# Attention and a two-layer product on one Trainium2 core: loads of five head pairs and weight pieces moved, and one unit's attention outputs and output product rearranged

## The chip, the cores and the metric

The kernel runs on one core of one Trainium2 chip. A core has five engines, each with its own instruction stream: TensorE (PE: matmuls; its weight loads are shown as PEld), VectorE (DVE), ScalarE (ACT), GpSimd (POOL) and SyncE (SP, which here only issues DMA). DMA is issued from SP's and from POOL's streams. An engine takes its instructions in order and waits on semaphores for what other engines and DMAs produce. Matmuls write into PSUM, which has eight banks of 2 KB per partition; DVE, ACT and POOL move data on from there or from SBUF.

The metric is the device time of one execution in microseconds (us), as the median of several runs. A profiled execution gives the trace of every instruction; its span reaches from the first to the last instruction, and its own time is a little longer.

## The reference

Attention over 8 batches, 12 heads, 448 tokens and 64 columns per head, and then a product with an elementwise function and a second product over all 3584 tokens:

```python
# q, k, v: (8, 12, 448, 64)
scale = 1.0 / np.sqrt(q.shape[-1])
scores = scale * np.matmul(q, k.transpose(0, 1, 3, 2))
m = np.max(scores, axis=-1, keepdims=True)
e = np.exp(scores - m)
attn = e / (np.sum(e, axis=-1, keepdims=True) + np.exp(-m) + 1e-09)
attn_out = np.matmul(attn, v)

x = attn_out.transpose(0, 2, 1, 3).reshape(8 * 448, 768)
h = x @ w_in                                  # (768, 2048)
sp = np.where(h > 20.0, h, np.log1p(np.exp(np.minimum(h, 20.0))))
g = h * np.tanh(sp)                           # mish
return g @ w_out                              # (2048, 768)
```

Inputs and output are float32; the kernel computes its matmuls in bf16.

## The kernel before

**Pairs, units, steps.** Two heads form a pair: 48 pairs, six per batch. Three pairs form a unit (`UNIT_PAIRS`), two units a batch (`UNITS_PER_B`). Pairs 0 to 5 are done in a head loop of their own. The main loop runs over u = 2, 3, ... (so u=4 is the fifth unit of pairs and u=5 the sixth). Each u has an attention block of 12 steps (n = 0 to 11: three pairs with four steps each, `STEPS`) and then an MLP block of eight tiles (f = 0 to 7). The attention block of u handles pairs 3u to 3u + 2; the MLP block of u handles batch (u − 2) // 2, whose attention has been done by then.

**A step.** `scores` multiplies q and k for two row tiles into one of three score tiles of PSUM (two banks each: sc0, sc1, sc2) and DVE takes the negative row maximum (L293). `exps` lets ACT take the exponentials (L306) into the bf16 buffer en and sum them. `scores_ahead` keeps up to three score tiles in use ahead of the exps. The remaining two PSUM banks (mo0, mo1) are handed out by `mo_take`, first free first, to everything else.

**Normalise and turn.** `denominators` forms the reciprocal of the sum. `normalise` scales en's seven tiles: by DVE (L341), by POOL (L339, `on_pool`, for the third pair of a unit), or shared in the head (tiles 0 to 3 by POOL, 4 to 6 by DVE). POOL reads its own copy of the reciprocals, rden2, which DVE makes (L331). en is then turned into eT, for most pairs by a DMA transpose on SP's queue (L345), for pairs 2, 4, 5, 6 and 7 by TensorE (`turn_on_pe`, L356, `BY_PE`). The three pairs of a unit are normalised in its MLP block, at f = 0, 3 and 4.

**Attention outputs.** `av_pair` multiplies eT and v in eight matmuls (L382), into a mo bank or into a bank it is given, and appends the copy to xT (L391) to a list, `late`, that `flush_late` empties at the next step. From u=4 on `av_with` is set: the output of the pair three back is put in at the last step of the current pair (`s == STEPS - 1`), in `scores`, into the second bank of the score tile, which that step does not use. That tile is free once the exps three steps earlier have read it. In u=2 and u=3 the table `AV_AT` puts the outputs at the ends of given steps, into mo banks. At u=4 the three outputs are those of pairs 9, 10 and 11.

**First product.** `mm1_mish`: six matmuls of xT with a tile of w_in (L406), then mish on ACT (L412). The bank is a mo bank, or for f = 1 the first score tile's. `transpose_pair` (L193) and `evac_qk` (L214, L227) prepare the next unit's q and k in the MLP block at f = 1, 3 and 5.

**Second product.** `mm2_part(g, i, q0, nq)`: row tile i (128 rows) of the two batches 2g and 2g + 1, and nq quarters of 192 columns from q0: 16 matmuls (L472) in eight chunks, a mo bank, and a copy by DVE (L459). `plan` lists which parts run in which u, from `first_mm2` = 4 on, as filler in the attention block: after the exps of step n the chunks due by `weight` (5.2 at n = 0, 1.0 for n = 1 to 8, 0.4 for the last three) are issued. Row tile 3 takes its rows from two batches; `gather_mid` (L422, DVE) copies 64 rows of each into one tile, mid, at the end of the unit with the batch's last first-product tiles.

**Queues.** SP's queue takes, in program order: `load_pair` (q, k and v of a pair, 224 KB each, L132), the DMA transposes, and the stores. Loads of pair p0 + 4, p0 + 5 and p0 + 6 (p0 = 3u) are issued at n = 0, 3 and 6 (`LOAD_AT`); there are four buffers for each of q, k and v. POOL's queue takes the casts to bf16 (`cast_pair` at n = 0, 3, 6, of the pair loaded before: L175, L176, L162), its share of the normalising, small copies, and the DMA issues of the weight pieces (`load_w`, L158): 12 pieces of w_in (256 KB), then 8 of w_out (384 KB; 12 to 15 are the first half of its columns, 16 to 19 the second). `W_AT` gives the steps of u = 2, 3 and 4 at which a piece is issued; in u=2 one more is issued at f = 2 and at f = 6.

Of the kernel before, what the change touches and what calls it, by code (L numbers as in the profile page):

```python
# [19 lines left out]
def kernel(  # L20
# [9 lines left out]
    nc = tc.nc  # L30
# [10 lines left out]
    NTILE = 2 * S // 128  # L41
    UNITS_PER_B = HP // UNIT_PAIRS
# [69 lines left out]
    def flush_late():  # L112
        while late:
            late.popleft()()
# [8 lines left out]
    def load_pair(p, which="qkv"):  # L123
        if p >= N_PAIRS:
            return
        b, h0 = p // HP, (p % HP) * 2
        tiles = loaded.setdefault(p, [])
        for nm, src in (("q", q), ("k", k), ("v", v)):
            if nm not in which:
                continue  # L130
            t = ld_pool.tile([SP_, 2, NT * D], FP32, tag=f"{nm}_f", name=f"{nm}_f")
            nc.sync.dma_start(  # L132
                out=t, in_=src[b, h0 : h0 + 2].rearrange("h (p t) d -> p h (t d)", t=NT)
            )
            tiles.append(t)
# [19 lines left out]
    def load_w(n):  # L155
        for _ in range(min(n, len(pieces))):
            dst, src = pieces.popleft()
            nc.gpsimd.dma_start(out=dst, in_=src.rearrange("(a p) c -> p a c", p=128))  # L158
# [80 lines left out]
    def scores_ahead(limit):  # L239

        while rg["next"] < limit and rg["used"] < len(sc_tiles):
            rg["used"] += 1
            scores(rg["next"])
            rg["next"] += 1
# [73 lines left out]
    def denominators(st):  # L318
        nc.vector.scalar_tensor_tensor(
            out=st["den"], in0=st["sums"], scalar=1e-9, in1=st["expm"],  # L320
            op0=ALU.add, op1=ALU.add,
        )
        nc.vector.reciprocal(out=st["rden"], in_=st["den"])

    def normalise(p, dma=True, on_pool=False, shared=0):
        st = att[p]
        en = st["en"]
        if on_pool or shared:

            st["rden2"] = st_pool.tile([128, NTILE], FP32, tag="rden2", name="rden2")  # L330
            nc.vector.tensor_copy(out=st["rden2"], in_=st["rden"])  # L331
        for i in range(NTILE):
            pool_does = on_pool or i < shared
            args = dict(
                out=en[:, :, i, 0:SP_], in0=en[:, :, i, 0:SP_],
                scalar1=st["rden2" if pool_does else "rden"][:, i : i + 1],
            )
            if pool_does:
                nc.gpsimd.tensor_scalar(scalar2=1.0, op0=ALU.mult, op1=ALU.mult, **args)  # L339
            else:  # L340
                nc.vector.tensor_scalar(scalar2=None, op0=ALU.mult, **args)  # L341
        eT = eT_pool.tile([128, NT, 2 * S], BF16, tag="eT", name="eT")
        st["eT"] = eT
        if dma:
            nc.sync.dma_start_transpose(  # L345
                out=eT.rearrange("c j (i q) -> c (j i) q", q=128),
                in_=en.rearrange("q j i c -> q (j i c)"),
            )
# [64 lines left out]
        if not spare:  # L413
            mo_free.append(h_ps)

    def gather_mid(b):

        g, half = divmod(b, 2)
        if half == 0:
            mids[g] = mid_pool.tile([128, FF_T, 128], BF16, tag="mid", name="mid")  # L420
        at = S - 64 if half == 0 else 0
        nc.vector.tensor_copy(  # L422
            out=mids[g][:, :, 64 * half : 64 * half + 64], in_=gT[b][:, :, at : at + 64]
        )

# [59 lines left out]
    first_mm2 = 2 * UNITS_PER_B  # L485

    def whole(g, i):
        return [(g, i, 0, 2), (g, i, 2, 2)]
# [3 lines left out]
    plan = {}  # L492
    for g in range(B // 2):
        u0 = first_mm2 + 4 * g
        rest = plan.pop(u0, [])
        if g == 0:
            plan[u0] = [(0, i, 0, 2) for i in range(2)] + [(0, 2, 0, 1)]
            plan[u0 + 1] = [(0, 2, 1, 1)] + [(0, i, 2, 2) for i in range(3)]
        else:
            plan[u0] = rest + whole(g, 0) + [(g, 1, 0, 1)]  # L500
            plan[u0 + 1] = [(g, 1, 1, 1), (g, 1, 2, 2)] + whole(g, 2)
        plan[u0 + 2] = [(g, 4, 0, 2), (g, 4, 2, 1)] + whole(g, 3)
        plan[u0 + 3] = [(g, 4, 3, 1)] + whole(g, 5) + [(g, 6, 0, 2)]
        if g < B // 2 - 1:
            plan[u0 + 4] = [(g, 6, 2, 2)]
        else:
            plan[u0 + 3] += [(g, 6, 2, 1), (g, 6, 3, 1)]
# [4 lines left out]
    BY_POOL = 4  # L512
    LEAD = UNIT_PAIRS + 1
    LOAD_AT = (0, 3, 6)
    LAST_AV_AT = (0, 6, 9)
    HEAD = HP

# [9 lines left out]
    }  # L527
    AV_HEAD = {(3, 3): 0, (4, 2): 2, (4, 3): 1}
    W_HEAD = {0: 3, 1: 1, 3: 1, 4: 1}
    AV_AT = ({3: 4, 7: 3, 9: 5}, {5: 6, 8: 7, 10: 8})  # L530

    W_AT = ({5: 1, 9: 1}, {1: 1, 4: 1, 5: 1, 7: 1, 9: 1, 11: 1}, {3: 1, 5: 1, 7: 1, 9: 1})
    for which in ("qk", "v"):
        for p in range(UNIT_PAIRS):
            load_pair(p, which)
# [12 lines left out]
    for p in range(HEAD):  # L548
        for s in range(STEPS):
# [20 lines left out]
            if (p, s) in AV_HEAD:  # L570
                av_pair(AV_HEAD[p, s], act=True)
    denominators(att[HEAD - 1])
    normalise(HEAD - 1, dma=HEAD - 1 not in BY_PE, shared=BY_POOL)

    for u in range(UNITS_PER_B, N_UNITS + 2 * UNITS_PER_B):
        attn = u < N_UNITS
        filler = deque()
        for part in plan.get(u, []):
            filler.extend(mm2_part(*part))
        total, done, acc = sum(w for _, w in filler), 0, 0.0  # L580
        p0 = u * UNIT_PAIRS
        if attn and u >= first_mm2:
            av_with.update({p0 + i: p0 + i - UNIT_PAIRS for i in range(UNIT_PAIRS)})
        end = min((u + 1) * UNIT_PAIRS, N_PAIRS) * STEPS

        for n in range(steps):
            pi, s = divmod(n, STEPS)
            p, idx = p0 + pi, p0 * STEPS + n
            late_tp = u == UNITS_PER_B and n == STEPS
            if late_tp:  # L590
                transpose_pair(p0 + 2)
            exps(idx)
            if late_tp:
                evac_qk(p0 + 2)
            if u == UNITS_PER_B + 1:
                for part in TURN_AT[1].get(n, []):
                    turn_on_pe(*part)
            flush_late()
            acc += weight[n]
            want = int(total * acc / sum(weight) + 1e-6)  # L600
            while done < want:
                fn, w = filler.popleft()
                fn()
                done += w
            scores_ahead(end)
            if n in LOAD_AT:
                load_pair(p0 + LOAD_AT.index(n) + LEAD)
                cast_pair(p0 + LOAD_AT.index(n) + LEAD - 1)
            if u - UNITS_PER_B < len(AV_AT):
                early = AV_AT[u - UNITS_PER_B]  # L610
                if n in early:
                    av_pair(early[n])
                if u == UNITS_PER_B:
                    for part in TURN_AT[0].get(n, []):
                        turn_on_pe(*part)
            elif u == N_UNITS and n in LAST_AV_AT:
                av_pair(p0 - UNIT_PAIRS + LAST_AV_AT.index(n))
            if u - UNITS_PER_B < len(W_AT):
                load_w(W_AT[u - UNITS_PER_B].get(n, 0))
        assert done == total  # L620

        moe = u < N_UNITS + UNITS_PER_B
        b, w = (u - UNITS_PER_B) // UNITS_PER_B, u % UNITS_PER_B
        nxt = p0 + UNIT_PAIRS
        todo = sorted(range(p0, nxt), key=lambda p: p in BY_PE)
        for f in range(FF_U):
            if moe:
                mm1_mish(b, w * FF_U + f)
            if u == UNITS_PER_B and f in (2, 6):
                load_w(1)  # L630
            if not attn:
                continue
            if f == 0:
                denominators(att[p0]["whole"])
                normalise(todo[0], dma=todo[0] not in BY_PE)
            if f in (1, 3, 5):
                transpose_pair(nxt + f // 2, bank=f // 2 % 2)
                evac_qk(nxt + f // 2)
            if nxt < DIAG_FROM and f in (4, 6):
                scores_ahead(nxt * STEPS + f // 2 - 1)  # L640
            if f == FF_U - 1:
                scores_ahead(min(nxt * STEPS + 3, N_PAIRS * STEPS))
            if f == 3:
                normalise(todo[1], dma=todo[1] not in BY_PE)
            if f == 4:
                normalise(todo[2], dma=todo[2] not in BY_PE, on_pool=True)
        if attn and u + 1 < N_UNITS:

            nc.scalar.activation(out=one, in_=zero, func=AF.Exp)
        if moe and w == UNITS_PER_B - 1:  # L650
            gather_mid(b)
    flush_late()
    assert not pieces and all(have == 4 for _, have in o_sbs.values())
# [30 lines left out]
```

## Time and profile before

| | |
|---|---|
| Median of three runs | 480.3 us (480.15 to 481.88) |
| The profiled execution's own time | 479.95 us |
| Its span, first to last instruction | 478.0 us |
| Instructions in the span | 8924 |
| Mean granted TensorE clock | 0.982 |
| PE busy (3064 matmuls) | 443.1 us |
| ACT busy | 350.0 us |
| DVE busy | 339.1 us |
| POOL busy | 181.1 us |

A page of the profile gives first the busy time of each engine, then 40 equal slices of the span in which a digit is the busy share in tenths, the granted TensorE clock (PEclk, also in tenths of full speed) and the DMA engines' share. Then comes the chain of work that ended last, followed back from the last instruction. An answer of the trace for windows gives, for stretches of the span, each engine's busy time with its number of instructions in brackets, the granted clock, the DMA share and the rate. A timeline row gives start, duration, engine, source line, operation, output and inputs, shape, the number of instructions put together, and in square brackets the engine's idle time in front and what ended it. Line numbers are those of the kernel before; in the changed kernel the lines behind `normalise` are six or more higher.

### The profile page before, as it was taken

The page shows a single profiled execution, that of the slowest core. Times are in us where ns is not written, and L with a number is a line of the kernel's source. Part 1 is how long each engine was busy: PE and PEld are TensorE (multiplying, and loading weights), DVE is VectorE, ACT ScalarE, POOL GpSimd, SP SyncE. Part 2 cuts the span into 40 slices and gives each one's busy share as a digit, 9 for nine tenths or more (in the row PEclk, how much of TensorE's full clock was granted, in tenths as well). Part 3 has the DMA queues.
Part 4 walks back from the last instruction along what each step waited for, and adds up shares of the span by engine and source line. Part 5 has one row for each costly group of instructions (what it writes and reads, how often), then busy time and mean ns, then how long its engine had stood idle before and what let it go on. Part 6 is the DMA issues. An engine that isn't in the chain of part 4 may idle for free.

```text
span 478.0 us, 8924 instructions
## 1 busy us (share of the span) xinstructions
PE 443.1 (93%) x3064; PEld 248.6 (52%) x3064; DVE 339.1 (71%) x680; ACT 350.0 (73%) x919; POOL 181.1 (38%) x315
## 2 busy tenths in 40 slices
PE   4565888898999999999999999999999999999997
PEld 2233544454655555555555555556555555556565
DVE  4888987968787886878687878788787869420021
ACT  5979678878787888979787878888897978412300
POOL 4877809255514334353535242433535340300000
PEclk9998798899999999999999999999999999999999
DMA  8999969999999989899999999899989595870113
GB/s 228 220 233 220 235 100 234 162 187 238 207 217 276 206 212 219 213 203 246 193 250 182 225 167 228 211 207 234 201 233 212 156 178 127 135 164 24 43 28 105
DMA packets 202381, 90.37 MB, mean 189 GB/s; under 512 B 159072, under 2 KB 198880, under 8 KB 202336
## 3 DMA queue, kind: packets, MB, share of 16 engines
q1 hardware_dynamic: 194848, 83.51, 81.3%
q0 software_dynamic: 7488, 6.29, 8.6%
q8 instruction: 24, 0.39, 0.3%
q14 instruction: 21, 0.17, 0.1%
HBM read 45.61 MB, written 11.01 MB: 118 GB/s over the span
## 4 chain that ended last, share of the span: by engine, by line
PE 76%; ACT 10%; DVE 9%; issue 2%; DMA 1%; POOL 0%; SPq 0%; DVEq 0%; ACTq 0%; POOLq 0%
PE mo L472 26%; PE mo L406 25%; ACT en L306 9%; PE sc L382 6%; DVE negm L293 6%; PE sc L266 5%; PE sc L406 4%; PE sc L193 3%; PE sc L272 2%; PE mo L356 1%; PE mo L382 1%; DVE en L341 1%; PE sc L280 1%; DVE eT L360 1%; DMA k_f<-in_k_dram 1%
## 5 line engine op out<-in xcount | busy, mean ns | idle before, releaser
L306 ACT ACTIVATE en<-sc,negm 128x448 bf16<-128x448 f32 x336 | 209.6, 637 | 26.4 <-DVE xT L391 10.4
L293 DVE TENSOR_REDUCE negm<-sc 128x2 f32<-128x896 f32 x192 | 180.7, 968 | 55.8 <-PE sc L275 26.0
L472 PE MATMUL mo<-w_out_sb,gT 128*128 128x384 bf16 (+1 forms) x912 | 142.3, 301 | 0.0
L406 PE MATMUL mo<-xT,w_in_sb 128*128 128x448 bf16 x672 | 137.7, 353 | 0.6 <-DVE xT L391 0.6
L412 ACT ACTIVATE gT<-mo 128x448 bf16<-128x448 f32 x112 | 61.3, 547 | 68.2 <-PE mo L406 68.1
L472 PEld LDWEIGHTS <-gT 128*128 128x128 bf16 x912 | 84.1, 98 | 48.2 <-issue 5.7
L339 POOL TENSOR_SCALAR en<-en,rden 128x448 bf16<-128x448 bf16 x122 | 76.4, 646 | 80.7 <-DVE rden L331 76.9
L406 PEld LDWEIGHTS <-w_in_sb 128*128 128x128 bf16 x768 | 72.9, 98 | 64.0 <-issue 3.0
L306 ACT ACTIVATION_READ_ACCUMULATOR en<-sc,negm 128x1 f32 x336 | 69.3, 206 | 0.0
L175 POOL CAST q_bf<-q_f 112x512 bf16<-112x512 f32 x47 | 29.0, 617 | 98.4 <-DMA q_f<-in_q_dram 98.0
L341 DVE TENSOR_SCALAR en<-en,rden 128x448 bf16<-128x448 bf16 x214 | 58.6, 345 | 0.9
L459 DVE COPY o_sb<-mo 128x384 f32<-128x384 f32 (+1 forms) x65 | 32.2, 495 | 35.1 <-PE mo L472 34.8
L266 PE MATMUL sc<-kT,qd 128*128 128x448 bf16 x168 | 47.7, 354 | 0.3 <-ACT en L306 0.2
L272 PE MATMUL sc<-kT,qd 64*128 64x448 bf16 x72 | 25.1, 411 | 12.7 <-ACT en L306 11.1
L382 PE MATMUL sc<-eT,v_bf 112*64 112x448 bf16 x288 | 34.1, 357 | 1.9 <-ACT en L306 1.7
L162 POOL CAST v_bf<-v_f 112x512 bf16<-112x512 f32 x48 | 29.5, 616 | 9.7 <-DMA v_f<-in_v_dram 8.8
L382 PEld LDWEIGHTS <-v_bf 112*64 112x64 bf16 x384 | 21.0, 112 | 22.8 <-issue 13.6
L176 POOL CAST k_bf<-k_f 112x512 bf16<-112x512 f32 x47 | 28.9, 616 | 7.5 <-DMA k_f<-in_k_dram 7.0
L227 DVE TENSOR_SCALAR qd<-sc 64x448 bf16<-64x448 bf16 x48 | 18.7, 389 | 11.9 <-PE sc L193 11.2
L266 PEld LDWEIGHTS <-qd 128*128 128x128 bf16 x168 | 16.3, 97 | 18.0 <-issue 9.2
L275 PE MATMUL sc<-kT,qd 64*128 64x448 bf16 x72 | 25.4, 415 | 0.0
L472 PE MATMUL mo<-w_out_sb,mid 128*128 128x384 bf16 x128 | 24.9, 326 | 0.0
(57 smaller groups left out, 340.1 us busy)
## 6 DMA issues: line engine op xcount, KB each, us to landing
q_f<-in_q_dram SPq DMA_DIRECT2D x48, 224.0 KB, 5.1
k_f<-in_k_dram SPq DMA_DIRECT2D x48, 224.0 KB, 5.4
v_f<-in_v_dram SPq DMA_DIRECT2D x48, 224.0 KB, 5.7
w_in_sb<-in_moe_w_in_dram POOLq DMA_DIRECT2D x12, 256.0 KB, 6.1
w_out_sb<-in_moe_w_out_dram POOLq DMA_DIRECT2D x8, 384.0 KB, 7.6
out_dram<-o_sb SPq DMA_DIRECT2D x7, 336.0 KB, 3.3
out_dram<-o_sb SPq DMA_DIRECT2D x8, 288.0 KB, 4.6
out_dram<-o_sb SPq DMA_DIRECT2D x8, 240.0 KB, 2.9
```

Source lines behind the costliest of these rows:

```text
L162: nc.gpsimd.tensor_copy(out=casted[p][2], in_=loaded.pop(p)[2])
L266: nc.tensor.matmul(sc[:, bk, 0:S], lhsT=qT[:, i].rearrange("d h r -> d (h r)"), rhs=kT, start=True, stop=True,)
L272: nc.tensor.matmul(sc[:, 0, 0:S], lhsT=qT[0:64, qa : qa + 128], rhs=kA, start=True, stop=True)
L293: nc.vector.tensor_reduce(out=negm, in_=sc[:, 0 : len(cols), 0:S], axis=AX.X, op=ALU.max, negate=True)
L306: nc.scalar.activation(out=st["en"][:, :, c, 0:SP_], in_=sc[:, bk, 0:S].rearrange("q (j c) -> q j c", j=NT), func=AF.Exp, bias=st["negm"][ ...
L339: nc.gpsimd.tensor_scalar(scalar2=1.0, op0=ALU.mult, op1=ALU.mult, **args)
L341: nc.vector.tensor_scalar(scalar2=None, op0=ALU.mult, **args)
L382: nc.tensor.matmul(av[h * 64 : (h + 1) * 64, 0:S], lhsT=v_bf[:, h, j * D : (j + 1) * D], rhs=e_h, start=(j == 0), stop=(j == NT - 1),)
L406: nc.tensor.matmul(h_ps[:, 0:S], lhsT=w_in_sb[:, dm, ff * 128 : (ff + 1) * 128], rhs=xT[b][:, dm, :], start=(dm == 0), stop=(dm == DM_T - 1),)
L412: nc.scalar.activation(out=gT[b][:, ff, :], in_=h_ps[:, 0:S], func=AF.Mish)
L459: nc.vector.tensor_copy(out=o_sb[:, cols], in_=st["o"][:, 0:n_cols])
L472: nc.tensor.matmul(st["o"][:, 0:n_cols], lhsT=src[:, ff, c0 : c0 + 128], rhs=w_out_sb[:, ff, cols], start=(ff == 0), stop=(ff == FF_T - 1),)
```

## The change

Five things are edited:

1. `normalise`, shared by DVE and POOL: for pairs 0 and 1 DVE does its tiles 4, 5 and 6 first, then makes rden2, and then POOL does tiles 0 to 3. The other shared pairs keep their order.
2. Loads: pairs 13 to 18 are issued by a table, `LOADS`. Pair 13 at n = 9 of u=2 and 14 at f = 1 of u=2 (before: n = 0 and 3 of u=3), 15 at n = 0 of u=3 (before: n = 6), 16 at n = 10 and 17 at f = 4 of u=3 (before: n = 0 and 3 of u=4), 18 at f = 1 of u=4 (before: n = 6). The one at f = 4 of u=3 is issued ahead of the last of that block's three DMA transposes.
3. Weight pieces: in u=2's MLP block both at f = 2; in u=3 at n = 1, 2, 4, 5, 7, 9; in u=4 two at n = 4, one at n = 5 and one at f = 1 (before: n = 3, 5, 7, 9).
4. u=4: `av_with` is not set; the outputs of pairs 9, 10 and 11 are put in at the ends of steps 3, 7 and 10 into mo banks. The second product gets six quarters there (three parts of two) where it had five, and u=5 gets six where it had seven; the two parts of one quarter become one of two. All second-half columns are then used from u=5 on.
5. The first `gather_mid`, of batch 0, moves from the end of u=3 on DVE to step 8 of u=5 on POOL.

```diff
@@ normalise @@
-        if on_pool or shared:
-
+        def for_pool():
             st["rden2"] = st_pool.tile([128, NTILE], FP32, tag="rden2", name="rden2")
             nc.vector.tensor_copy(out=st["rden2"], in_=st["rden"])
-        for i in range(NTILE):
+        order = list(range(NTILE))
+        if shared and p < 2:
+            order = order[shared:] + order[:shared]
+        for i in order:
+            if i == 0 and (on_pool or shared):
+                for_pool()
             pool_does = on_pool or i < shared
@@ gather_mid @@
-    def gather_mid(b):
+    def gather_mid(b, copy=nc.vector.tensor_copy):
...
-        nc.vector.tensor_copy(
+        copy(
@@ plan @@
-            plan[u0] = [(0, i, 0, 2) for i in range(2)] + [(0, 2, 0, 1)]
-            plan[u0 + 1] = [(0, 2, 1, 1)] + [(0, i, 2, 2) for i in range(3)]
+            plan[u0] = [(0, i, 0, 2) for i in range(3)]
+            plan[u0 + 1] = [(0, i, 2, 2) for i in range(3)]
@@ tables @@
+    W_MISH = {(2, 2): 2, (4, 1): 1}
+    LOADS = {
+        2: ({0: 10, 3: 11, 6: 12, 9: 13}, {1: 14}),
+        3: ({0: 15, 10: 16}, {4: 17}),
+        4: ({}, {1: 18}),
+    }
...
-    AV_AT = ({3: 4, 7: 3, 9: 5}, {5: 6, 8: 7, 10: 8})
-
-    W_AT = ({5: 1, 9: 1}, {1: 1, 4: 1, 5: 1, 7: 1, 9: 1, 11: 1}, {3: 1, 5: 1, 7: 1, 9: 1})
+    AV_AT = ({3: 4, 7: 3, 9: 5}, {5: 6, 8: 7, 10: 8}, {3: 9, 7: 10, 10: 11})
+
+    W_AT = ({5: 1, 9: 1}, {1: 1, 2: 1, 4: 1, 5: 1, 7: 1, 9: 1}, {4: 2, 5: 1})
@@ main loop @@
-        if attn and u >= first_mm2:
+        if attn and u > first_mm2:
             av_with.update({p0 + i: p0 + i - UNIT_PAIRS for i in range(UNIT_PAIRS)})
@@ at the end of a step @@
+            if u in LOADS:
+                if n in LOADS[u][0]:
+                    load_pair(LOADS[u][0][n])
+            elif n in LOAD_AT:
+                load_pair(p0 + LOAD_AT.index(n) + LEAD)
             if n in LOAD_AT:
-                load_pair(p0 + LOAD_AT.index(n) + LEAD)
                 cast_pair(p0 + LOAD_AT.index(n) + LEAD - 1)
...
+            if (u, n) == (first_mm2 + 1, 8):
+                gather_mid(0, nc.gpsimd.tensor_copy)
@@ MLP block @@
-            if u == UNITS_PER_B and f in (2, 6):
-                load_w(1)
+            if (u, f) in W_MISH:
+                load_w(W_MISH[u, f])
+            if u in LOADS and f in LOADS[u][1]:
+                load_pair(LOADS[u][1][f])
...
-        if moe and w == UNITS_PER_B - 1:
+        if moe and w == UNITS_PER_B - 1 and b > 0:
             gather_mid(b)
```

In the MLP block the `load_w` and `load_pair` lines stand behind `mm1_mish` and ahead of that f's `normalise`.

## The prediction, made before the changed kernel had run

> **What bounds the kernel now.** I read the page's busy shares and 40 slices first, then its chain of waits, then a table of windows by stage, then the timelines of PE, SP, POOL and DVE in the stages that are touched. The page:
>
> ```profile
> PE 443.1 (93%) x3064; PEld 248.6 (52%) x3064; DVE 339.1 (71%) x680; ACT 350.0 (73%) x919; POOL 181.1 (38%) x315
> ...
> PE   4565888898999999999999999999999999999997
> ...
> PEclk9998798899999999999999999999999999999999
> DMA  8999969999999989899999999899989595870113
> ...
> PE 76%; ACT 10%; DVE 9%; issue 2%; DMA 1%; POOL 0%; SPq 0%; DVEq 0%; ACTq 0%; POOLq 0%
> ```
>
> One digit is 11.95 us. PE is full from the eleventh slice on; ACT and DVE have shares in the chain only ahead of it. So time can be taken only ahead of about 155 us, and only where PE idles. Now the windows by stage (length, busy us of PE, PEld, DVE, ACT and POOL, granted clock, DMA share, GB/s):
>
> ```profile
> 75.30:78.67 3.37, 1.21 (x18) 0.97 (x17) 2.00 (x4) 3.34 (x10) 3.36 (x7) 1.00 0.89 257
> 78.67:82.08 3.41, 3.29 (x25) 2.25 (x22) 3.25 (x5) 3.36 (x12) 3.41 (x7) 0.50 1.04 234
> 85.50:88.91 3.41, 1.88 (x20) 1.10 (x19) 3.41 (x6) 2.06 (x8) 1.19 (x2) 1.00 1.27 191
> 88.91:92.32 3.41, 3.41 (x19) 1.36 (x14) 2.73 (x5) 3.39 (x12) 0.00 (x0) 0.50 1.32 203
> 102.89:117.73 14.84, 12.91 (x89) 7.27 (x88) 13.14 (x17) 13.57 (x41) 7.67 (x13) 1.00 1.07 229
> ...
> 128.77:143.81 15.04, 15.02 (x106) 8.50 (x105) 12.69 (x17) 13.54 (x39) 4.68 (x9) 1.00 1.08 226
> 143.81:155.51 11.70, 11.20 (x79) 5.98 (x78) 8.70 (x26) 8.54 (x20) 5.65 (x11) 1.00 1.22 273
> 155.51:170.46 14.95, 14.95 (x105) 8.48 (x104) 13.36 (x18) 13.46 (x39) 5.45 (x10) 1.00 1.02 225
> ```
>
> The fifth unit (u=4) has its attention block at 102.89–117.73: PE is idle for 14.84 − 12.91 = 1.93 us, with ACT at 13.57. The sixth (u=5) is full in attention (7 quarters) and loses 11.70 − 11.20 = 0.50 us in its MLP block. The seventh (6 quarters) is the pattern wanted: 14.95, full. So all that can be had behind 102 us is 1.93 + 0.50 = 2.43 us. The first four rows show what idle PE costs: windows in which PE works 1.21 and 1.88 of 3.4 us are followed by one at clock 0.50. Where u=4 loses its 1.93 us (start, duration, then the idle time in front and its releaser):
>
> ```profile
> 105.67 0.95 PE L382 MATMUL sc<-eT,v_bf 112*64 112x448 bf16 x8 [0.32 <-ACT en L306]
> ...
> 111.06 0.95 PE L382 MATMUL sc<-eT,v_bf 112*64 112x448 bf16 x8 [0.83 <-ACT en L306]
> ...
> 115.99 0.95 PE L382 MATMUL sc<-eT,v_bf 112*64 112x448 bf16 x8 [0.52 <-ACT en L306]
> ...
> 117.07 0.82 PE L472 MATMUL mo<-w_out_sb,gT 128*128 128x192 bf16 x8
> ```
>
> Three attention outputs stand in score banks and wait for the exps that free them: 0.32 + 0.83 + 0.52, and 0.21 more at a score at 114.44, is 1.88 of the 1.93.
>
> **The change part by part.**
>
> *Outputs into mo banks (u=4).* The three waits go. No work is removed. An output in a mo bank is copied by the same L391 copy (0.61 us). The third, two product matmuls ahead of the MLP block, leaves its bank to the MLP's first tile; the same hand-over at 63.40 us shows 0.58 us idle "<-DVE xT L391". Two matmuls, 0.33 us together (next paragraph), lie between, so 0.25 to 0.58; I take 0.4.
>
> *Six quarters instead of five (u=4), six instead of seven (u=5).* The row at 117.07 starts eight matmuls of 192 columns, and the MLP block starts at 117.73: 0.66 / 8 = 0.083 us each (0.165 with 384 columns). One quarter is 16 of them: 1.3 us. It leaves u=5 and enters u=4. Two evacuations of 192 columns become one of 384, off the path. u=4: 12.91 + 1.3 + 0.4 = 14.6 against 14.84, so −0.2 (bounds: −0.63, with no hand-over wait, to +0.3, where ACT and DVE set 14.84 anyway and the hand-over comes on top). u=5's attention: 15.04 − 1.3 = 13.74 if PE alone set it. But u=5 keeps the score-bank outputs, with ACT at 13.54 and DVE at 12.69 of busy time, and the one block of before with so little product work, u=4, could not go below 14.84. With six quarters PE has 13.7 us of work, nearer to u=4's 12.91 than to 15.02, so I take 14.6: −0.45 (bounds −1.3 to 0).
>
> *Loads and weights.* Now SP (waits of the queue itself) and POOL:
>
> ```profile
> 95.03 13.69 SPq L345 DMA_TRANSPOSE eT<-en  x3
> ```
> ```profile
> 112.06 0.62 POOL L175 CAST q_bf<-q_f 112x512 bf16<-112x512 f32 x1 [5.93 <-DMA q_f<-in_q_dram]
> ...
> 115.09 1.55 POOL L158 DMA_DIRECT2D w_out_sb<-in_moe_w_out_dram  x2
> ```
>
> Loads for u=5, due early in u=4, leave only behind the three transposes of pairs 9 to 11 (the last issue ends at 108.72), and POOL waits 5.93 us for them. Issued up to a unit sooner, they let POOL's casts run without it; POOL's weight pieces then leave at about 107.8, where they left at 115.09. In u=2 and u=3 the moved issues (about 0.5 us each on SP, 0.78 on POOL) stand behind transposes that are not needed for microseconds: nothing, with ±0.2 for the two half-clock windows lying in u=3. In u=5 the DMA traffic comes about 4 us sooner, and the casts of its loads leave the place where they lie now, beside a DVE block:
>
> ```profile
> 149.41 0.36 PE L193 MATMUL sc<-ident,q_bf 112*128 112x112 bf16 x4 [0.51 <-DVE qd L214]
> ```
> ```profile
> 146.09 2.97 DVE L341 TENSOR_SCALAR en<-en,rden 128x448 bf16<-128x448 bf16 x7
> ...
> 150.63 1.81 DVE L341 TENSOR_SCALAR en<-en,rden 128x448 bf16<-128x448 bf16 x7
> ```
>
> The same seven tiles take 1.81 us at 150.63 and 2.97 while POOL casts at 146.66 to 148.7; qd is late by that, and PE loses 0.51. With the casts gone I take −0.5 (bounds −0.5 to 0).
>
> *The first gather* leaves DVE at 105.63 (0.78 us) for POOL in u=5. POOL rows of 64 elements take 0.23 us and of 448 take 0.65, so 1024 is about 1.3 us by the line through them. No one needs it before u=6: nothing; if it lies beside L341, up to +0.3.
>
> *DVE's tiles first (pairs 0 and 1).* DVE starts the same work; POOL's four tiles start up to 0.8 us later (three tiles take 0.82 us), and the transposes behind them too. In the head ACT sets the pace (slices of 5 to 9 with PE at 4 to 8) and these outputs are used 10 us later. Nothing, ±0.3.
>
> *Sum:* −0.2 − 0.45 − 0.5 = −1.15 us on the profiled 479.95 (span 478.0 and 1.95 outside it) is 478.8. The median of the three runs is 0.35 above that execution, so on it 479.15; I say **479.2**.
>
> **Where it could go wrong: the transposes.** A moved load is in front of the last transpose: three issues, about 1.5 us, so that of pair 11 leaves at about 105.9, not 104.48. Alone it takes 6.2 us (112.1). But three weight pieces now leave in its flight. Where a piece was issued beside a transpose, the answer for one start reads:
>
> ```profile
> w_in_sb<-in_moe_w_in_dram POOLq DMA_DIRECT2D x1, 256.0 KB, 7.3
> eT<-en SPq DMA_TRANSPOSE x1, 9.2
> ```
>
> The piece, issued 1.6 us behind, lands just ahead of it. A w_out piece is about 2.1 us of transfer (an estimate: of u=4's four, the first lands at 121.7 and the last at 128.1, 6.4 / 3), so behind one, two or three pieces the transpose lands at 114.2, 116.3 or 118.4. Its output matmuls are due at 117.5 − 0.4 − 0.33 − 0.95, about 115.8. I take one to two pieces: landing by 116, no stall that counts. The Trainium skill ("DMA: Bandwidth & Descriptors", section "Queues, rings and completion order") says that each DMA engine alternates between its queues packet by packet; by that the 4.3 us left at 107.8 run at half speed, it lands at about 116.4, and the sum would be 479.8; the 9.2 agrees. It also says that a completion is written only after all earlier writes of that engine, which speaks for the late end.
>
> **Rivals.**
>
> (a) *Everything that can be had:* u=5 is PE-bound too, no hand-over wait. −0.63 − 1.3 − 0.5 = −2.43: 477.9. For it: u=6's 14.95 has no idle time at six quarters. Against: the same row needs PE at 14.95, where u=5 will have 13.7.
>
> (b) *Slower: pair 11's transpose late in u=4.* PE runs in order; the output waits and the MLP block, which needs it, stands behind. Landing at 118.4 the stall is 2.6 us; one of more than about 1.4 us can halve the clock for a window of 3.41 us, as after 85.50, another 1.7. 2.6 + 1.7 − 1.15 = +3.15: 483.5; without the clock 481.8. It decides from a landing behind about 117 us (stall equal to the gains). Against: 115.8 leaves 3.7 us over the lone transpose's 112.1, one piece took 3.0 of them (9.2 − 6.2), and what POOL issues after about 110 may start too late to count. On the clock the Trainium skill ("TensorE: Matmul & The Clock Gate", section "HAM oscillation — how this bites in real kernels") has idle gaps above some 3.4 us as the limit; the rows above show less to be enough, and by the skill's limit the rival would give 481.8 at most.
>
> (c) *Nothing gained:* ACT and DVE hold u=5 at 15, and casts or gather fall on L341 again: −0.2 to +0.2, 480.3. That the loads aren't sooner (buffers not free: four per kind) would end here as well.
>
> **How the numbers follow.** About 0.5% (2.4 us) is what a measurement of this kernel tells from no change. Forecast 0.50, (a) 0.13, (b) 0.24, (c) 0.13. Of (a) most reaches the bound, 0.10, and 0.02 comes from elsewhere: faster 0.12. Of (b) the half with the clock passes it, 0.13, and unnamed losses in u=2 and u=3, where PE idles already, 0.05: slower 0.18. The rest, 0.70, is within. The likeliest case's own range is 478.3 to 480.2; to leave out no more than 2 in 10 it reaches to (a), 477.8, and to most of (b), 483.2.
>
> **What would show it.** u=4's attention window near 14.6 with PE at 14.2 and no "<-ACT en" in front of L382's successor; its third output waiting for the copy or nothing (forecast), or for "DMA eT" (b). u=5's window at 13.8 (a), 14.6, or 15 (c). L341 of pair 15 at 1.8 and no idle time in front of L193. POOL's 5.93 gone. The granted clock at 1.00 from 103 us on. Wrong is the forecast if the median leaves 478.3 to 480.2, and its frame, that only u=4 and u=5 matter, if the MLP start of u=4 moves by more than its own window does.

## The result and the profile after

The changed kernel takes 481.92 us (median of 20, 480.72 to 485.23) against 480.48 (median of 20, 479.39 to 482.37) for the kernel before on the same chip: a ratio of 1.0036, 95% interval 1.0022 to 1.005. It is slower by 1.1 to 2.4 us, where 1.15 us faster was forecast; 481.92 lies inside the stated range.

The profiled execution took 483.78 us. Its page, with the same lines as before (busy time of the engines, PE's slices, the chain by engine):

```profile
PE 444.9 (92%) x3048; PEld 247.6 (51%) x3048; DVE 338.0 (70%) x678; ACT 349.6 (73%) x919; POOL 181.3 (38%) x316
...
PE   4566888898998999999999999999999999999997
...
PE 72%; DVE 9%; ACT 8%; DMA 5%; POOL 3%; issue 2%; SPq 0%; DVEq 0%; POOLq 0%; ACTq 0%
```

The engines' work is the same to within 2 us. The chain is not: DMA had 1% of it and POOL 0%, and now they have 5% and 3%. A transfer, and what feeds it, has come onto the path. The windows of u=4's attention block, its MLP block, and u=5's attention block (columns as before):

```profile
102.85:120.29 17.44, 14.95 (x94) 7.22 (x94) 13.77 (x18) 16.56 (x47) 10.24 (x17) 1.00 1.23 191
120.29:130.66 10.37, 10.37 (x74) 5.78 (x73) 6.45 (x23) 5.22 (x10) 2.52 (x6) 1.00 1.02 192
130.66:146.41 15.75, 14.41 (x94) 7.55 (x94) 12.79 (x16) 14.11 (x42) 5.19 (x9) 1.00 1.11 217
```

u=4's attention block was 14.84 us and is 17.44: PE is idle for 2.49 us in it, more than the 1.93 before, with a quarter more of work. u=5's, with a quarter less, is longer than its 15.04 too. (Both blocks begin sooner after the MLP start ahead of them than they did, u=4's by 1.1 us and u=5's by 0.7, so the distances from MLP start to MLP start, below, are the fair comparison.) PE's timeline names the waits:

```profile
107.53 0.54 PE L266 MATMUL sc<-kT,qd 128*128 128x448 bf16 x2 [0.39 <-DVE negm L293]
...
118.62 0.95 PE L388 MATMUL mo<-eT,v_bf 112*64 112x448 bf16 x8 [1.77 <-DMA eT<-en]
...
120.29 1.30 PE L412 MATMUL mo<-xT,w_in_sb 128*128 128x448 bf16 x6 [0.29 <-DVE xT L397]
...
139.29 0.95 PE L388 MATMUL sc<-eT,v_bf 112*64 112x448 bf16 x8 [0.60 <-ACT en L306]
144.68 0.95 PE L388 MATMUL sc<-eT,v_bf 112*64 112x448 bf16 x8 [0.74 <-ACT en L306]
152.56 0.36 PE L193 MATMUL sc<-ident,q_bf 112*128 112x112 bf16 x4 [1.05 <-DVE qd L214]
```

The third output of u=4, pair 11's, waits 1.77 us for its transpose; a score ahead of it waits 0.39 for DVE, and the MLP block 0.29 for the output's copy. u=5, which had no idle PE in attention, now waits 0.60 and 0.74 for exps in front of its score-bank outputs. In u=5's MLP block the wait for qd grew from 0.51 to 1.05. The queues behind the first wait (SP, then POOL, then the answer for the start of that one transpose):

```profile
104.81 0.53 SPq L132 DMA_DIRECT2D q_f<-in_q_dram  x1
105.43 0.42 SPq L132 DMA_DIRECT2D k_f<-in_k_dram  x1
105.94 0.41 SPq L132 DMA_DIRECT2D v_f<-in_v_dram  x1
106.46 20.67 SPq L351 DMA_TRANSPOSE eT<-en  x2
```
```profile
108.39 2.30 POOL L158 DMA_DIRECT2D w_out_sb<-in_moe_w_out_dram  x3
```
```profile
eT<-en SPq DMA_TRANSPOSE x1, 12.1
```

Pair 17's load is issued first, the transpose at 106.46, the three weight pieces two microseconds behind it. The transpose takes 12.1 us (6.2 before) and lands at 118.6; PE had been ready at 118.62 − 1.77 = 116.85.

One execution's sum is coarse, because in the head the half-clock windows fall differently each time: u=3's MLP block starts at 91.42 in the trace of before and at 92.49 here, between 90.9 and 94.9 in all traces, and at 92.53 and 91.26 in two traces of one and the same kernel (x10 and x16, below). So the units are compared by the distance from one MLP block's first matmul to the next one's. Three traces have the order of before from u=2 on (before, and two of an experiment that alters the head alone), and three that of the change (the changed kernel twice, and once without its head part):

| us from MLP start to MLP start | as before | changed | means |
|---|---|---|---|
| u=3 to u=4 | 26.31, 25.87, 25.87 | 27.80, 27.95, 27.50 | +1.73 |
| u=4 to u=5 | 26.08, 26.63, 26.36 | 26.12, 26.13, 26.12 | −0.23 |
| u=5 to u=6 | 26.65, 26.66, 26.43 | 27.20, 26.86, 27.29 | +0.54 |
| u=7 to u=8 | 26.16, 26.16, 26.16 | 26.50, 26.52, 26.51 | +0.35 |

The other distances behind u=3 agree within 0.02. The sum is +2.4 us, at the upper end of the measured +1.1 to +2.4. The 26.31 of the trace of before holds 0.9 us at half clock (91.42 to 92.32), some 0.45 us of loss that the other two traces do not have. And the three traced executions of the change (483.78, 483.16 and 483.21 us) are all slower than their kernels' medians (481.92, and 482.24 for the one without the head part), so the table tells where these three lose time; how much of each loss the median execution has, no trace shows.

### The profile page after: what moved, and what is told of

Its sections match the earlier page's. It is cut to its first block, busy times and chain, and to the rows that moved or that the text cites. A ratio compares the mean times of both kernels' runs of the same rounds, so it can differ in the third digit from the quotient of the medians.

```text
span 481.6 us, 8894 instructions
## 1 busy us (share of the span) xinstructions
PE 444.9 (92%) x3048; PEld 247.6 (51%) x3048; DVE 338.0 (70%) x678; ACT 349.6 (73%) x919; POOL 181.3 (38%) x316
## 4 chain that ended last, share of the span: by engine, by line
PE 72%; DVE 9%; ACT 8%; DMA 5%; POOL 3%; issue 2%; SPq 0%; DVEq 0%; POOLq 0%; ACTq 0%
PE mo L478 26%; PE mo L412 24%; ACT en L306 6%; PE sc L388 6%; PE sc L266 5%; DVE negm L293 5%; PE sc L412 3%; PE sc L193 3%; DMA eT<-en 3%; PE sc L272 2%; DVE en L347 2%; POOL en L345 2%; PE mo L388 1%; DMA w_out_sb<-in_moe_w_out_dram 1%; PE mo L362 1%
## 5 line engine op out<-in xcount | busy, mean ns | idle before, releaser
L478 PEld LDWEIGHTS <-gT 128*128 128x128 bf16 x896 | 82.7, 98 | 49.7 <-issue 7.0
L272 PE MATMUL sc<-kT,qd 64*128 64x448 bf16 x72 | 25.9, 421 | 12.4 <-ACT en L306 11.8
L162 POOL CAST v_bf<-v_f 112x512 bf16<-112x512 f32 x48 | 29.5, 615 | 11.9 <-DMA v_f<-in_v_dram 10.6
L388 PE MATMUL sc<-eT,v_bf 112*64 112x448 bf16 x264 | 31.3, 357 | 1.9 <-ACT en L306 1.8
L227 DVE TENSOR_SCALAR qd<-sc 64x448 bf16<-64x448 bf16 x48 | 18.7, 389 | 12.9 <-PE sc L193 12.2
L275 PE MATMUL sc<-kT,qd 64*128 64x448 bf16 x72 | 26.2, 426 | 0.0
```

The source lines that it names most:

```text
L162: nc.gpsimd.tensor_copy(out=casted[p][2], in_=loaded.pop(p)[2])
L272: nc.tensor.matmul(sc[:, 0, 0:S], lhsT=qT[0:64, qa : qa + 128], rhs=kA, start=True, stop=True)
L388: nc.tensor.matmul(av[h * 64 : (h + 1) * 64, 0:S], lhsT=v_bf[:, h, j * D : (j + 1) * D], rhs=e_h, start=(j == 0), stop=(j == NT - 1),)
L478: nc.tensor.matmul(st["o"][:, 0:n_cols], lhsT=src[:, ff, c0 : c0 + 128], rhs=w_out_sb[:, ff, cols], start=(ff == 0), stop=(ff == FF_T - 1),)
```

## The experiments

Times are medians; ratios are to the kernel before on the same chip, with 95% intervals.

**x1, part 4 alone, and x5, parts 2 and 3 alone.** x1 is the kernel before with the diff's lines of `plan`, `AV_AT` and `av_with`; x5 is the changed kernel with these, the gather and the head order undone.

> The kernel before with part 4 of the change alone: in u=4 the outputs of pairs 9 to 11 in mo banks and six quarters, in u=5 six quarters; loads, weight pieces, gather and head as before. Theory A (the loss of the change comes from pair 11's DMA transpose, which a load was put in front of and weight pieces beside): here the transpose lands about 6.2 us after its issue at about 104.5, so the third output waits for no DMA, the distance from u=3's MLP start to u=4's is 26.1 (26.31 before, 27.80 in the changed kernel), and the time is 0.2 to 0.8 us below before. Rival B (the six quarters and the mo banks themselves cost it, with ACT and DVE as the bound): the distance stays above 27 with no DMA wait, and the time is 1 us or more above before. From u=4's to u=5's MLP start both expect about 26.1, since the changed kernel had 26.12 there (26.08 before) with PE waiting 0.60 and 0.74 for the exps.

> The kernel before with parts 2 and 3 of the change alone (loads of pairs 13 to 18 and weight pieces); outputs, quarters, gather and head as before. Theory A (load ahead and pieces beside pair 11's transpose make it late whatever the outputs do): the transpose lands at about 118 again; its output, in a score bank and due at about 116, waits about 2 us for DMA; the distance from u=3's MLP start to u=4's is 27.5 to 28.5 (26.31 before). Rival: the transpose is late only because six quarters and the mo-bank outputs draw the stages together; then it lands by 116 and the distance stays at 26.3. From u=7's to u=8's MLP start it should be 26.16 as before, since every kernel with the six quarters has 26.51 there and this one has not.

x1: 481.48 us, 1.0027 (1.0008 to 1.0047). u=3 to u=4 took 25.96 with no DMA wait, as theory A has it, but the kernel is slower all the same: u=4 to u=5 took 28.22. There the weight pieces, issued as before at 115.6 to 119.6, are in flight with the transposes of u=4's MLP block; pair 12's took 11.7 us (9.3 before, 9.7 in x8, the kernel before with part 1 alone), and pair 13's, behind it, is late:

```profile
139.32 0.95 PE L382 MATMUL sc<-eT,v_bf 112*64 112x448 bf16 x8 [1.72 <-DMA eT<-en]
```

That was not expected. The change, which issues these pieces earlier, does not have it (26.12 in its traces); that the pieces are the cause is argued from this, as no run moved them alone in x1. x5: 482.02 us, 1.0027 (1.0003 to 1.0051); u=3 to u=4 27.72, the transpose 11.9 us. The loss is there without the mo-bank outputs or the sixth quarter, with a wait of 1.42 us where about 2 was expected (timeline of PE):

```profile
120.91 0.95 PE L387 MATMUL sc<-eT,v_bf 112*64 112x448 bf16 x8 [1.42 <-DMA eT<-en]
```

So parts 2 and 3 make the wait of u=4. From u=7 to u=8 it had 26.16, as expected.

**x2, x3 (and x12), x4: which transfer makes it late.**

```diff
@@ x2, x4 @@
-        3: ({0: 15, 10: 16}, {4: 17}),
+        3: ({0: 15, 10: 16}, {5: 17}),
@@ x3, x12, x4 @@
-    W_AT = ({5: 1, 9: 1}, {1: 1, 2: 1, 4: 1, 5: 1, 7: 1, 9: 1}, {4: 2, 5: 1})
+    W_AT = ({5: 1, 9: 1}, {1: 1, 2: 1, 4: 1, 5: 1, 7: 1, 9: 1, 11: 3})
```

> The changed kernel with pair 17's load issued at f=5 of u=3, behind pair 11's DMA transpose, not ahead of it; the weight pieces stay beside the transpose. In the changed kernel the transpose was issued at 106.46 and landed at 118.58, 12.1 us later, and the output waited 1.77 us. Theory A1 (the load ahead is the main cause: it holds the queue until 110.05): issue at about 104.9, landing by about 113, no wait, distance u=3 to u=4 26.3, time 1.5 us below the changed kernel. Rival A2 (the weight pieces are the main cause): the transpose still takes 9 to 12 us, landing 114 to 117, the wait falls only from 1.77 to between 0 and 0.5, and the three tensors of the load take their share of the engines behind it.

> The changed kernel with the three weight pieces of u=4's steps 4 and 5 issued at step 11 of u=3, ahead of the three DMA transposes; pair 17's load stays ahead of the last transpose. Theory A1 (load): the transpose of pair 11 is issued at about 106.5 or later and lands 6.2 us after the load's end at about 110, at 116 or more, so the wait is 0 to 1 us. Theory A2 (pieces): it lands at 112.7 to 114, no wait, distance u=3 to u=4 26.3, time 1.5 us below the changed kernel. The price to look for: the transposes of pairs 9 and 10 land up to 6 us later than 102.4 and 106.61, behind three pieces of about 2 us each; their outputs are due at 110.3 and 114.6.

> The kernel with the pieces ahead and the load still ahead of the transpose, once more: its one trace showed no wait (transpose landed 116.11, its output due at about 116) at 480.71 us, but its other times were 481.85 to 484.74. If the landing stands on the edge, this trace may show 0 to 1 us of wait, and the times spread from 480.5 to 483; if those times came from elsewhere (a second half-clock window in the head or u=3), the trace shows it there, with no wait in u=4.

> The changed kernel with both: pair 17's load behind pair 11's transpose and the three pieces at step 11 of u=3. Theory A: no DMA wait in u=4, distance u=3 to u=4 26.2 to 26.4, time 1.5 to 1.8 us below the changed kernel and 0 to 0.3 us from before. If the distance stays above 27 with no DMA wait in front of the third output, theory A falls. u=5 is expected at 26.1 with the waits for exps of 0.6 and 0.74 us left, since nothing here touches them.

Times: x2 481.05 us, 1.0009 (0.9996 to 1.0022); x3 483.55 us, 1.0063 (1.0038 to 1.0088); x12, the same kernel again, 483.86 us, 1.0072 (1.0051 to 1.0093); x4 480.54 us, 1.0009 (0.9996 to 1.0022).

| | load ahead | pieces beside | issue of pair 11's transpose | its duration | wait | u=3 to u=4 |
|---|---|---|---|---|---|---|
| changed, two traces | yes | yes | 106.46, 106.41 | 12.1, 12.2 | 1.77, 1.91 | 27.80, 27.95 |
| x2 | no | yes | 104.69 | 7.9 | none | 25.95 |
| x3 and x12 | yes | no | 106.45, 108.62 | 9.7, 9.7 | none, 2.40 | 26.40, 28.44 |
| x4 | no | no | 106.7 | 6.1 | none | 25.96 |

(Issue, duration and wait in us, issues by each trace's own clock; without either it takes the 6.1 to 6.2 it took before. The 26.40 holds the same half-clock stretch as the 26.31 of before.) The pieces beside it cost the transpose 1.7 us, the load in front 3.5, both 5.9. The 3.5 is a bound from above: in x3 and x12 the fourth weight piece was issued during the transpose (110.53 and 112.99), and no run has the load in front without any piece. Moving the load behind is enough (theory A1). Moving the pieces alone is no better than the change: ahead of pair 9's transpose they delay the whole queue, pair 11's is issued 2 us later in the second trace than in the first, and the wait is 2.40, where 0 to 1 was expected. There the clock follows. PE's timeline, and windows of 3.40 us, of x12:

```profile
118.39 0.95 PE L388 MATMUL mo<-eT,v_bf 112*64 112x448 bf16 x8 [2.40 <-DMA eT<-en]
```
```profile
116.00:119.40 3.40, 1.01 (x9) 0.48 (x10) 0.42 (x2) 3.17 (x8) 0.00 (x0) 1.00 0.74 103
119.40:122.80 3.40, 3.32 (x10) 1.29 (x9) 3.32 (x11) 0.31 (x1) 0.00 (x0) 0.50 0.01 1
```

The window behind the wait runs at 0.50, and u=4 to u=5 takes 27.47, 1.35 us more than the change. In the traces of the change, with 1.47 to 1.91 us of wait, the clock stayed at 1.00.

x2 and x4, with no late transpose, are still not faster than before. The next three experiments ask why.

**x9, the quarters alone.** The kernel before with the two changed lines of `plan` and nothing else, so u=4's outputs stay in score banks.

> The kernel before with the quarters alone: six in u=4, six in u=5; the outputs of u=4 stay in score banks, loads, pieces, gather and head as before. In the kernel before, u=4 had five quarters and 25.87 us from u=3's MLP start at full clock (26.31 in the execution shown, with 0.9 us of it at half clock); with six quarters and mo-bank outputs it had 25.95, PE's idle time falling from 1.93 to 0.72 while its work rose by 1.3. Theory F (ACT's chain of exps sets the attention block; PE's idle time in it is only the rest, so a quarter is free there and the outputs' banks give nothing): 25.9 to 26.2 here, with PE idle in front of the score-bank outputs 0.3 to 0.6 us in all. Rival G (the score-bank waits were a cost, and the mo banks are what pays for the quarter): 1.3 us more than 25.87, about 27.1. In both, u=5 is 26.1 or, with a transpose late behind the weight pieces, up to 28.

481.06 us, 1.0021 (1.0009 to 1.0034). u=3 to u=4: 26.12 (theory F). PE's timeline in u=4:

```profile
113.30 0.95 PE L382 MATMUL sc<-eT,v_bf 112*64 112x448 bf16 x8 [0.60 <-ACT en L306]
118.69 0.95 PE L382 MATMUL sc<-eT,v_bf 112*64 112x448 bf16 x8 [0.74 <-ACT en L306]
```

With a quarter more the distance grew by 26.12 − 25.87 = 0.25 us. PE's busy time in it rose from 23.94 us (x8) to 24.77, less than the 1.3 of the prediction's count, and its idle time fell from 1.93 to 1.35, not to the 0.3 to 0.6 expected. The waits are those of u=5 in the changed kernel to the hundredth: both blocks have six quarters and outputs in score banks. What sets them is not ACT alone. The chain of the attention block, followed back from its end, is 53% ACT with five quarters (before, u=4); in x9 it is 18% ACT, 29% DVE and 49% PE: an output waits for exps, the next score for that output, DVE's maximum for that score, and the next exps for the maximum. The mo banks are worth 26.12 − 25.96 = 0.16 us: in x1 PE is idle for only 0.72 us, but its busy time for the same matmuls is 25.24, not 24.77; why, no run showed. (u=5 lost 0.90 us here to a transpose late behind the weight pieces, as in x1.)

**x6, the gather's place, and x7, u=5's outputs in mo banks.** On x4:

```diff
@@ x6, x7 @@
-            if (u, n) == (first_mm2 + 1, 8):
+            if (u, n) == (first_mm2 + 1, 2):
@@ x7 @@
-    AV_AT = ({3: 4, 7: 3, 9: 5}, {5: 6, 8: 7, 10: 8}, {3: 9, 7: 10, 10: 11})
+    AV_AT = ({3: 4, 7: 3, 9: 5}, {5: 6, 8: 7, 10: 8}, {3: 9, 7: 10, 10: 11}, {3: 12, 7: 13, 10: 14})
-        if attn and u > first_mm2:
+        if attn and u > first_mm2 + 1:
```

> The kernel with the load behind and the pieces ahead, and in it the first gather on POOL at step 2 of u=5, not step 8. There u=5's MLP block lost 1.04 us in front of the q transposes, with DVE's seven tiles at 3.50 us beside POOL's casts and the gather (1.04 us at 147.3). If the gather's place is what the block lost over before (0.51): tiles at about 3.0, idle 0.5, the distance u=5 to u=6 falls from 27.2 to 26.7 and the time by 0.5 us. Rival: the casts alone do it, in which case the distance stays above 27.

> The same kernel as x6, and in it u=5's outputs (pairs 12 to 14) in mo banks at steps 3, 7 and 10, as u=4's. If u=5 stayed at 26.12 with a quarter less because of the exps in front of the two outputs in score banks (0.60 and 0.74 us), the distance u=4 to u=5 falls by 0.9 to 1.3 us, to about 25.0, no transpose being due later than its landing (127.7, 133.7, 138.7 against steps at about 130, 136 and 140). Rival: ACT or DVE set u=5 as a whole, with PE idle somewhere else in place of it: 25.8 to 26.1. In the time: 480.0 to 480.5 for the rival, 479.0 to 479.5 for the theory, where before is 480.3.

x6: 479.72 us, 0.9986 (0.9965 to 1.0008); u=5 to u=6 26.48, with 0.33 us of idle time. In the changed kernel DVE and then POOL had:

```profile
148.88 3.33 DVE L347 TENSOR_SCALAR en<-en,rden 128x448 bf16<-128x448 bf16 x7
```
```profile
149.25 0.62 POOL L162 CAST v_bf<-v_f 112x512 bf16<-112x512 f32 x1
149.81 1.04 POOL L428 COPY mid<-gT 128x1024 bf16<-128x1024 bf16 x1
```

and in x6, where POOL gathers at 131.37, DVE has:

```profile
145.77 2.54 DVE L347 TENSOR_SCALAR en<-en,rden 128x448 bf16<-128x448 bf16 x7
```

The seven tiles take 1.81 us alone, 2.54 beside part of the casts, 3.33 beside casts and gather. So the gather's place accounts for the loss of this block.

x7: 479.46 us, 0.9982 (0.9964 to 1.0), in the range that the theory gave. The traces say otherwise: the waits of 0.60 and 0.74 are gone, but u=4 to u=5 takes 25.96, not 25.0: the rival. (u=5 to u=6 took 25.99, 0.49 less than in x6, which nobody expected; its cause is open.) A window from MLP start to MLP start shows what became of the quarter that left:

```profile
118.39:144.35 25.96, 25.24 (x166) 12.98 (x165) 20.21 (x41) 21.76 (x59) 8.67 (x15) 1.00 0.97 199
```

PE is idle for 0.72 us (0.39 before a score that waits for DVE, 0.29 before the MLP block), with ACT at its exps without a gap over 0.5 us through the attention block. The chain of that block is 70% PE and 25% DVE, with no exp in it. So six quarters and mo banks give 25.96, and seven with score banks and no wait give 26.00 in the later units: taking the quarter out won next to nothing in either form. PE and ACT are both nearly full there, and no run tells which of them is the floor.

**x10 and x16, four tiny DVE instructions.** In x7, behind the first fill of `zero`:

```diff
     nc.vector.memset(zero, 0.0)
+    for _ in range(4):
+        nc.vector.memset(one, 0.0)
```

> The kernel of x7 with four tiny DVE fills (128x1 each) added at the start; nothing else. From u=7's to u=8's MLP start every kernel with six quarters has 26.47 to 26.51, those without 26.15: in the one kind DVE pauses 0.3 us behind an output's copy in u=8 with nothing to wait for, in the other some instructions earlier. Theory (the pause belongs to a place in DVE's instruction stream, and moves with the number of instructions ahead): the distance falls to 26.15 or the pause moves to another place. Rival (it is tied to the work of u=8 or to a transfer): 26.47 again at the same place.

> The kernel of x10 once more (load behind, pieces ahead, gather at step 2, u=5's outputs in mo banks, four tiny DVE fills), beside x15: 0.9961 to 0.9989 of before if the first comparison holds.

The +0.35 of u=7 to u=8 appears in all kernels so far with six quarters in u=4 but x9 (26.16), though no work of u=8 differs. DVE's timeline there, before and in x4:

```profile
215.65 1.09 DVE L293 TENSOR_REDUCE negm<-sc 128x2 f32<-128x896 f32 x1 [0.29 <-issue]
216.66 0.55 DVE L459 COPY o_sb<-mo 128x384 f32<-128x384 f32 x1
217.14 0.62 DVE L293 TENSOR_REDUCE negm<-sc 128x1 f32<-128x448 f32 x1
```
```profile
216.47 0.55 DVE L465 COPY o_sb<-mo 128x384 f32<-128x384 f32 x1
217.66 0.62 DVE L293 TENSOR_REDUCE negm<-sc 128x1 f32<-128x448 f32 x1 [0.64 <-PE sc L266]
```

Before, DVE pauses 0.29 us ahead of one maximum, with nothing to wait for, and has slack there. In x4 the pause stands two instructions later, ahead of a maximum that ACT is waiting for; its score had ended at 217.2, and where there is no pause such a maximum starts 0.1 us behind its score. With four instructions more at the start, x10 has 26.15 again, and x16 too, where x7 had 26.47: so the pause moves with the instructions ahead of it. The page has 680 instructions on DVE before and 678 with the change, but this count does not decide alone: x1 and x9 both have 679, with 26.51 and 26.16. What the pause is, no run showed. (In its other units x10's trace lost 0.15 and 0.27 us, from u=5 to u=6 and from u=6 to u=7, that x16's did not.)

x10: 479.09 us, 0.9975 (0.9961 to 0.9989); x16: 479.06 us, 0.9973 (0.9958 to 0.9989). This version is faster than the kernel before by 0.1 to 0.4%.

**x8, x13, x14, x15: the head order (part 1).** x8 and x13 are the kernel before with part 1 alone, x14 the changed kernel and x15 the kernel of x10 without it. x11 is the changed kernel once more, for a second trace; its numbers stand above.

> The kernel before with part 1 alone (pairs 0 and 1: DVE's tiles first). Theory: within 0.3 us of before, since ACT sets the pace of the head; the first MLP start at 63.4 to 65 as the phase of the clock's windows falls. Rival: POOL's later start delays the loads and transposes behind it and costs 0.5 us or more.

> Part 1 alone once more: the first comparison gave 0.9982 of before, interval 0.9959 to 1.0005. Theory H (part 1 gains 0.5 to 1 us in the head): 0.998 to 0.999 with an interval below 1. Rival N (nothing in the head, as predicted): 0.9995 to 1.0005.

> The changed kernel without part 1 (pairs 0 and 1 in the order of before). Theory H: 0.5 to 1 us above the changed kernel, ratio to before 1.0045 to 1.006. Rival N: 1.0036, within its interval of 1.0022 to 1.005. The transpose of pair 11 late by 1.5 to 2.5 us in both.

> The kernel of x10 without part 1. Theory H: 0.5 to 1 us above x16 on the same chip. Rival N: within 0.3 us of x16.

> The changed kernel once more, for a second trace. In the first, pair 11's transpose took 12.1 us and the output waited 1.77; 20 times ranged from 480.7 to 485.2. If the wait belongs to the kernel: 1.3 to 2.3 us again, and the distance u=3 to u=4 27.3 to 28.3. If it was one execution's: below 0.5 us.

x8 479.75 us, 0.9982 (0.9959 to 1.0005); x13 480.18 us, 0.9993 (0.9975 to 1.001); x14 482.24 us, 1.0042 (1.0019 to 1.0064); x15 479.18 us, 0.9967 (0.995 to 0.9984) beside x16's 0.9973. No pair shows a difference (rival N), though one of 0.2%, about 1 us, is within the intervals. x11: 483.16 us and a wait of 1.91, so the wait belongs to the kernel.

## Why the prediction was wrong

- **The step that failed: "I take one to two pieces: landing by 116, no stall that counts."** The transpose landed at 118.6 in both traces of the changed kernel, and PE waited 1.77 and 1.91 us. The landing that the text priced for three pieces, 118.4, went into rival (b), at a chance of 0.24. The three issues of the load were taken as 1.5 us of queue time only; the load's 672 KB were left out of the transfer, and they cost up to 3.5 us (x3), twice what the pieces cost (1.7, x2). Without the late transpose (x2, x4) the loss of u=4 is gone.
- **Rival (b) without the clock, 481.8, is near the measured 481.92, but partly by luck.** Its mechanism is the one that the runs showed. Its sum is a stall of 2.6 us less 1.15 of gains; in the traces the stall is 1.5 to 1.9, the gains are all but absent, and two losses of 0.54 and 0.35 come on top.
- **The Trainium skill's rule** ("DMA: Bandwidth & Descriptors", section "Queues, rings and completion order") gave 116.4. That transfers of different queues share the engines agrees: three pieces on POOL's queue stretched the transpose on SP's from 6.2 us to 7.9 (x2). The working with half speed does not come out: it gives 9.1 us for x2 (2.9 us left when the pieces start) and 10.8 for the 9.2 that the prediction took as agreeing. With the times of this trace (issue at 106.46, pieces at 108.39) it gives a landing at 116.9, and 1.7 us are missing although it overstates the pieces; x2 leaves the load in front, in the same queue, for them.
- **"−0.2" in u=4** without the late transpose: 25.87 to 25.95, +0.1 (x2). The waits of 1.88 us went and PE's work grew by 1.3 us, as forecast, but PE's idle time fell only from 1.93 us to 0.72: beside the hand-over, 0.29, a score waits 0.39 for DVE, and this was not in the sum. Nor were the 1.88 us all to be had: with six quarters, taking away 1.34 us of waits at the score banks gave 0.16 (x9 against x1).
- **"−0.45" in u=5's attention**: nothing. 26.12 and 26.13 in the traces of the change, where before had 26.08 without a late transpose and 26.36, 26.63 with one. The quarter that left turned into 0.60 + 0.74 us of idle time. The sentence that u=4 "could not go below 14.84" held the answer; the middle between it and PE's work was no estimate of anything.
- **"The seventh (6 quarters)" was misread.** `plan` gives u=6 seven quarters, and its unit has the matmuls of seven. So no block of before ran six quarters without idle time, and what the text held for rival (a), "14.95 has no idle time at six quarters", was not there.
- **"−0.5" in u=5's MLP block**: +0.5. The loads of u=5 did not come 4 us sooner, as they still stand behind the transposes of u=4's MLP block (140.82, where it was 138.50; from that block's start 20.5 and 20.8 us), so the casts still fall beside DVE's tiles.
- **The gather at nothing, "+0.3" beside L341**: it did fall beside them, and the block lost 0.54 us (x6 gives it back).
- **Right:** part 1 and the moves of u=2 and u=3 at nothing, as far as the runs can tell; POOL's weight pieces leaving earlier (108.39 against 107.8); the hand-over in front of the MLP block (0.29, taken 0.4). Not foreseen: the +0.35 of DVE's pause, outside u=4 and u=5.

## What to carry to other kernels

Idle time of an engine inside a block may be only what a chain through the other engines leaves over: put more work into the block once, look whether it gets longer, and only then count the idle time as a gain. In front of a transfer that something waits for, count the bytes of what is moved ahead in its queue, and not only the time of the issue, and follow it to the instruction that needs it. Compare traces by distances within the steady part, with the clock's windows taken out, before reading a few tenths of a microsecond from one execution.

## What the runs showed of the hardware

- A window of 3.40 us in which PE worked 1.01 us, with a wait of 2.40 in it, was followed by one at half clock, while waits of 1.47 to 1.91 in other traces were not. The Trainium skill ("TensorE: Matmul & The Clock Gate", section "HAM oscillation — how this bites in real kernels") has gaps above some 3.4 us; here 2.40 was enough. The prediction's row at 85.50, with 1.53 us of idle time in the window, shows that less can be, while waits of up to 1.91 did not do it here: the length of one gap does not decide alone.
- Pair 11's DMA transpose takes 6.1 to 6.2 us alone, 7.9 beside three weight pieces, 9.7 behind a load of 672 KB in its queue (with one weight piece issued during it), and 11.8 to 12.2 with the load and three pieces.
- DVE pauses some 0.3 us with nothing to wait for, at a place that moves with the instructions ahead of it: four small ones more at the start took 26.47 us from u=7 to u=8 back to 26.15.
